# A cached-attention block on one core: one row in fourteen of the last weight matrix is loaded by a part of the DMA engines

## The chip, the core and the metric

The kernel runs on one core of one Trainium2 chip. Times are device microseconds (us) of whole executions; the figure for a kernel is the median of its runs. One execution was also taken with the hardware profiler: its span is counted from the first to the last instruction. TensorE (PE) multiplies matrices, VectorE (DVE) and ScalarE (ACT) work element by element, GpSimd (POOL) clears memory, SyncE (SP) issues the transfers, and 16 DMA engines move the data from memory (HBM) into the 128 partitions of the on-chip buffer.

## The reference, cut to what matters

A decoder block for 8 batch rows of width 512. Attention looks at the last 2048 keys of 8 cache heads in each of 8 batch rows (32 query heads of 128); its caches make up most of the bytes. Behind it stands an MLP: 512 to 1792 to 512, with a squared relu between. All is float32.

```
mod = (silu(c) @ w_mod).reshape(8, 6, 1, 512)      # sa, ca, ga, sb, cb, gb
h = layernorm(x) * (1 + ca) + sa
q = h @ wq                                          # 512 x 4096
o = softmax(q k^T / sqrt(128)) v                    # last 2048 positions of each cache
x = x + ga * (o @ wo)                               # 4096 x 512
h = layernorm(x) * (1 + cb) + sb
r = relu(h @ w1 + b1)                               # 512 x 1792
out = x + gb * ((r * r) @ w2 + b2)                  # 1792 x 512
```

## The kernel before

Every large array goes through four buffers, `slots`, of 128 partitions by 32 KB. A list `loads` (line 105) gives their order: w_mod and wq, then K and V of each batch row in two halves of 4 MB, then wo in two halves, w1 and w2. `pump` (line 115) hands the next entry to `load` (line 71) as soon as a slot is free, and `done` (line 120) frees one behind the last instruction that reads it. All these transfers are issued on SP's queue, in the order of the list, and a transfer waits at its issue for the slot's last readers. Two further things set when it is issued: the eight semaphores on which landings are counted go round, so a transfer also waits for the landing of the one eight issues before it.

The caches' middle part (lines 286 to 448) is a software pipeline over the eight batch rows: DVE transposes K in its slot (line 287), PE makes the scores (line 297), ACT the exponentials, PE the weighted sum of V (line 378). `qb` (line 206) are two buffers of 4 KB in a partition which hold the queries for line 297, spread with zeros; they are read last in the second half of the last batch row. The bytes of K, V, wo, w1 and w2 are spread over partitions so that every transfer into a slot has 128 of them.

What the change touches comes behind that. `wo` (line 453) is multiplied in two forms. Its first 16 row groups go 512 columns wide, four at a time into four groups of 32 columns of the array; their partial sums are copied to SBUF (lines 463 and 464) and folded in by line 467. The 16 others, loaded in pieces of 8, 4 and 4, go in the form of line 472: four matmuls of 128 columns for each row group. Then x1, its layernorm (`norm`, `scaled`) and the transposed `h2T` follow (lines 479 to 483).

The MLP: each partition holds four rows of w1 (`"(p kc) n -> p kc n"`), and 14 rows of w2 (`"(p c) n -> p c n"`). The first product has its 1792 columns cut in four parts of 448 (FG), one for each 32 columns of the array (line 494), after a matmul of four rows that puts the bias in (line 489). Relu, square and a transpose of 32 by 32 blocks (lines 505 to 507) run in two halves of seven, and make `rT`: 14 (FC) left operands of 128 by 32, one for each row of w2 in a partition. Line 516 multiplies each by its row of w2 in four parts of 128 columns, and y goes out (lines 524 to 526). w1 is loaded in two pieces (three of its four rows, then one) and w2 in pieces of 8, 4, 1 and 1 rows; PE waits for each piece by itself. b1 and b2 are loaded at the start, by POOL's queue.

## Time and profile before

| | |
|---|---|
| median of 3 runs | 394.1 us (393.8 to 394.24) |
| the profiled execution | 394.03 us, its span 392.2 us |
| mean granted TensorE clock in it | 0.839 |
| busy: PE, DVE, ACT, POOL | 65%, 55%, 11%, 1% of the span |
| moved by SP's queue (q1) | 164.69 MB in 6768 packets, 98.1% of the 16 engines' span |
| read from HBM | 164.77 MB, 420 GB/s over the span |

A row of a timeline gives start, duration, engine, line, operation, output and inputs, count, and in brackets how long the engine stood idle before it and for whom. A row of a table of windows gives the stretch, its length, the busy time of PE, PE's weight loads, DVE, ACT and POOL with the number of instructions, the granted TensorE clock, the share of the 16 DMA engines' time that was busy, and GB/s. PE shows two passes, so two instructions and two weight loads, for each float32 matmul of the source. The chain of waits is followed back from the last instruction.

### The profile page before, as it was taken

To read this page: it belongs to the slowest core of one execution; us is meant where nothing else is said; L and a number is where in the kernel's file an instruction comes from. 1 tells how busy PE (TensorE), PEld (TensorE's weight loads), DVE (VectorE), ACT (ScalarE), POOL (GpSimd) and SP (SyncE) were. 2 spreads that over 40 slices of the span, in tenths; PEclk is the share of its full clock that TensorE was granted. 3 is DMA by queue.
4 is the path that set the end of the run, shared out by engine and by line. 5 is a ranking of instruction groups with operands and counts; after the bars stand their busy time and mean duration, and the time that the engine had idled before them with its cause. 6 is when DMAs were issued, how large, how long until landed. Compare 5 with 4: busy or idle time off the path is not lost.

```text
span 392.2 us, 4985 instructions
## 1 busy us (share of the span) xinstructions
PE 254.6 (65%) x2224; PEld 112.9 (29%) x2224; DVE 213.8 (55%) x228; ACT 42.0 (11%) x88; POOL 4.7 (1%) x12
## 2 busy tenths in 40 slices
PE   0554808678966693849484939394849384984965
PEld 0211302051231332224332522143224221452423
DVE  2420299399394939283928491939293927230022
ACT  1300100030030002000200120003000300140000
POOL 4000000000000000000000000000000000000000
PEclk9998768969977988789578967797788879997869
DMA  8999999999999999999999999999999999999994
GB/s 333 429 428 426 431 441 438 431 434 438 426 431 426 428 426 428 428 433 434 429 434 433 438 427 428 434 433 428 426 428 434 424 431 426 438 429 412 433 417 170
DMA packets 6997, 165.15 MB, mean 421 GB/s; under 512 B 824, under 2 KB 1088, under 8 KB 1472
## 3 DMA queue, kind: packets, MB, share of 16 engines
q1 hardware_dynamic: 6768, 164.69, 98.1%
q8 instruction: 17, 0.28, 0.3%
q10 hardware_dynamic: 144, 0.13, 0.1%
q14 instruction: 4, 0.03, 0.0%
q0 software_dynamic: 64, 0.01, 0.0%
HBM read 164.77 MB, written 0.07 MB: 420 GB/s over the span
## 4 chain that ended last, share of the span: by engine, by line
DMA 55%; DVE 23%; PE 20%; issue 0%; ACT 0%; DVEq 0%; ACTq 0%
DMA slot<-in_A_k_cache_dram 37%; DVE slot L287 20%; PE s_ps L297 16%; DMA slot<-in_B_w_dram 8%; DMA slot<-in_A_v_cache_dram 6%; DMA xc_in<-in_xc_dram 3%; PE m_ps L221 2%; PE o_ps L378 2%; DVE pT L367 1%; PE t_ps L366 1%; PE t_ps L516 0%; DVE s L309 0%; DVE s L313 0%; DVE mx L318 0%; DVE e_sb L148 0%
## 5 line engine op out<-in xcount | busy, mean ns | idle before, releaser
L287 DVE STREAM_TRANSPOSE slot<-slot 128x2048 f32<-128x2048 f32 x64 | 144.0, 2284 | 43.4 <-DMA slot<-in_A_k_cache_dram 43.3
L297 PE MATMUL s_ps<-slot,qb 128*32 128x512 f32 x512 | 120.9, 1092 | 71.1 <-DVE slot L287 70.5
L297 PEld LDWEIGHTS s_ps<-slot,qb 128*32 128x32 f32 x512 | 24.2, 135 | 147.3 <-issue 79.0
L378 PE MATMUL o_ps<-slot,pT 128*32 128x256 f32 x1024 | 59.7, 381 | 0.8 <-DMA slot<-in_A_v_cache_dram 0.8
L378 PEld LDWEIGHTS o_ps<-slot,pT 128*32 128x32 f32 x1024 | 45.4, 112 | 29.1 <-issue 18.4
L366 PE MATMUL t_ps<-ident,prd 128*128 128x128 f32 x128 | 25.2, 348 | 17.3 <-ACT prd L356 9.5
L309 DVE STREAM_TRANSPOSE s<-s_ps 128x512 f32<-128x512 f32 x8 | 5.7, 717 | 54.1 <-PE s_ps L297 54.1
L366 PEld LDWEIGHTS t_ps<-ident,prd 128*128 128x128 f32 x128 | 18.5, 177 | 23.1 <-ACT prd L356 22.4
L356 ACT ACTIVATE prd<-pr,rz 128x512 f32<-128x512 f32 x32 | 20.5, 710 | 9.4 <-DVE rz L348 9.4
L332 ACT ACTIVATE pr<-s,nm 128x512 f32<-128x512 f32 x8 | 5.8, 722 | 142.7 <-DVE nm L326 142.7
L367 DVE TENSOR_TENSOR pT<-t_ps,m 128x512 f32<-128x512 f32 x32 | 20.2, 670 | 0.7 <-PE t_ps L366 0.6
L388 ACT COPY o_sb<-o_ps 128x256 f32<-128x256 f32 x16 | 5.8, 362 | 121.7 <-PE o_ps L378 121.7
L243 PE MATMUL t_ps<-slot,h1T 128*32 128x512 f32 x64 | 11.6, 889 | 10.2 <-DMA slot<-in_A_wq_dram 10.2
L255 DVE STREAM_TRANSPOSE qT<-t_ps 128x512 f32<-128x512 f32 x2 | 1.4, 717 | 19.0 <-PE t_ps L243 19.0
L274 DVE TENSOR_TENSOR qb<-qrep,block 128x512 f32<-128x512 f32 x8 | 9.0, 1124 | 2.1 <-ACT qrep L266 2.1
L158 PE MATMUL m_ps<-xsum,sel 128*128 128x1 f32 x2 | 0.6, 363 | 13.9 <-DVE xsum L181 13.9
L344 PE MATMUL m_ps<-z,same 128*128 128x1 f32 x16 | 3.3, 273 | 9.1 <-ACT pr L332 9.1
L453 PE MATMUL s_ps<-slot,oT 128*32 128x512 f32 x32 | 5.6, 864 | 5.2 <-DMA slot<-in_A_wo_dram 5.2
L243 PEld LDWEIGHTS t_ps<-slot,h1T 128*32 128x32 f32 x64 | 2.7, 155 | 18.6 <-issue 12.1
L221 PE MATMUL m_ps<-slot,cT 128*32 128x384 f32 x64 | 7.9, 665 | 0.0
L404 DVE TENSOR_TENSOR og<-m_ps,m 128x128 f32<-128x128 f32 x8 | 2.2, 272 | 8.9 <-PE m_ps L396 8.9
L494 PE MATMUL t_ps<-slot,h2T 128*32 128x448 f32 x32 | 5.6, 871 | 2.2 <-DMA slot<-in_B_w_dram 2.2
(93 smaller groups left out, 95.1 us busy)
## 6 DMA issues: line engine op xcount, KB each, us to landing
slot<-in_A_k_cache_dram SPq DMA_DIRECT2D x16, 4096.0 KB, 21.8
slot<-in_A_v_cache_dram SPq DMA_DIRECT2D x16, 4096.0 KB, 25.9
slot<-in_A_wq_dram SPq DMA_DIRECT2D x2, 4096.0 KB, 31.7
slot<-in_w_mod_dram SPq DMA_DIRECT2D x2, 3072.0 KB, 13.9
slot<-in_A_wo_dram SPq DMA_DIRECT2D x1, 4096.0 KB, 22.6
slot<-in_B_w_dram SPq DMA_DIRECT2D x1, 2688.0 KB, 27.8
slot<-in_A_wo_dram SPq DMA_DIRECT2D x1, 2048.0 KB, 25.7
slot<-in_A_wo_dram SPq DMA_DIRECT2D x2, 1024.0 KB, 28.2
```

What stands on the lines that cost most here:

```text
L221: nc.tensor.matmul(pm[i][32 * q : 32 * q + 32, : 3 * P].rearrange("p (m n) -> p m n", m=3), cT[:, kc, :], wm[:, 3 * i : 3 * i + 3, q, :], ...
L243: nc.tensor.matmul(pq[t][32 * x : 32 * x + 32, :], hT[:, kc, :], w[:, 2048 * t + 512 * x : 2048 * t + 512 * x + 512], start=(kc == 0), sto ...
L274: nc.vector.tensor_mul(qb[b % 2][:, :, :, :REP], qrep_b[:, :, None, :, b].to_broadcast([P, 32, 4, REP]), block[:, None, :, None].to_broadc ...
L287: nc.vector.transpose(k, k)
L297: nc.tensor.matmul(S_[b][32 * x : 32 * x + 32, :].rearrange("p (j i) -> p j i", i=8), q[:, n : n + 32], k[:, :, c, :, x], start=(t == 0 an ...
L309: nc.vector.transpose(s1.rearrange("p a j r -> p j a r"), S_.pop(b).rearrange("p (j i) -> p j i", i=32))
L332: nc.scalar.activation(pr.rearrange("p j (a i) -> p j a i", a=4), S2_.pop(b).rearrange("p (a j i) -> p j a i", a=4, i=8), AF.Exp, bias=NM_ ...
L356: nc.scalar.activation(d, pr[:, 4 * n : 4 * n + 4, :, None].to_broadcast([P, 4, 32, 4]), AF.Copy, scale=RZ_[b][0])
L366: nc.tensor.transpose(pp[:, P * i : P * i + P], d[:, i].rearrange("p i u -> p (i u)"), one)
L367: nc.vector.tensor_mul(PT_[b][:, n].rearrange("p q j (x r) -> p q (j x) r", r=REP), pp.rearrange("p (y q r) -> p q y r", y=16, r=REP), m16 ...
L378: nc.tensor.matmul(o[32 * (m % 4) : 32 * (m % 4) + 32].rearrange("p u d -> p (u d)"), PT_[b][:, n, 2 * q + t, 2 * u : 2 * u + 2, :].rearra ...
L388: nc.scalar.copy(O_[b][:, t], o)
```

## The change

w2's first 1664 rows are loaded as before, but 13 to a partition (FC is 13 and FG 416), in pieces of 6, 4, 1, 1 and 1. Its last 128 rows go to 32 partitions, four rows (8 KB) to each: 80 rows to partitions 0 to 19 and 48 rows to partitions 32 to 43. The access pattern of each of these two transfers has 5 and 3 as its outermost dimension; the change calls them loads of five and of three engines. They stand in SP's queue between w1 and the other pieces of w2. Their place is the memory of the two `qb` buffers, which are now one tile, `qb_all`; POOL clears 64 partitions of it behind the last scores (a memset of 64 by 2048), since the matmuls read 64 partitions.

w1 is loaded in four pieces instead of two. The 128 columns of w1 that belong to the extra rows of w2 have matmuls of their own, of 80 and of 48 columns, into another bank, `px`; relu, square and transpose of them make `rxT` with four left operands of 64 by 32, and 16 more matmuls of line 563 multiply them by `w2x` ahead of the others. Relu and square now run over 6 and 7 of the 13.

wo's form of 512 columns takes 28 row groups instead of 16, and the form of 128 columns the last four. b1 (in two parts) and b2 are issued on ACT's queue at the start, behind xc, instead of POOL's.

PE's program at wo, before (s_ps takes the form of 512 columns, m_ps that of 128; slot_81 holds wo's first half, slot_82 its second):

```order
L453 MATMUL s_ps<-slot_81,oT 32x512 x16
L467 MATMUL m_ps<-at_i,sel 32x128 x4
L472 MATMUL m_ps<-slot_82,oT 32x128 x64
L158 MATMUL m_ps<-x1sum,sel 128x1
L167 MATMUL m_ps<-ssq,sel 128x1
```

and the same place now (slot_84 and slot_85 are wo's halves):

```order
L470 MATMUL s_ps<-slot_84,oT 32x512 x16
L470 MATMUL s_ps<-slot_85,oT 32x512 x12
L484 MATMUL m_ps<-at_i,sel 32x128 x4
L489 MATMUL m_ps<-slot_85,oT 32x128 x16
L171 MATMUL m_ps<-x1sum,sel 128x1
L180 MATMUL m_ps<-ssq,sel 128x1
```

Twelve row groups went ahead of the fold, and 48 matmuls of 128 columns behind it became 12 of 512 ahead of it.

PE's program in the MLP, before (slot_84 is w1, slot_83 w2):

```order
L167 MATMUL m_ps<-ssq,sel 128x1
L489 MATMUL t_ps<-b_in,ident 32x448 x4
L494 MATMUL t_ps<-slot_84,h2T 32x448 x16
L511 MATMUL t_ps<-b_in,ident 32x128 x4
L516 MATMUL t_ps<-slot_83,rT 32x128 x56
```

and now (slot_87 is w1, slot_86 w2, qb_all the extra rows of w2; the three rows behind L511 stand four times, once for each row of w1):

```order
L507 MATMUL t_ps<-b_in,ident 32x416 x4
L511 MATMUL m_ps<-b_x,ident 32x80
L511 MATMUL m_ps<-b_x,ident 32x48
L520 MATMUL m_ps<-slot_87,h2T 32x80
L520 MATMUL m_ps<-slot_87,h2T 32x48
L528 MATMUL t_ps<-slot_87,h2T 32x416 x4
...
L556 MATMUL t_ps<-b_in,ident 32x128 x4
L563 MATMUL t_ps<-qb_all,rxT 32x128 x16
L563 MATMUL t_ps<-slot_86,rT 32x128 x52
```

The first product has ten matmuls more, the second twelve more, and the new sixteen stand first in the second.

SP's queue, its last transfers before with what each waits for (PE_49 is PE's count, a name with DMAHW an earlier landing; slot_82 is wo's second half, slot_84 w1, slot_83 w2):

```order
L99 DMA slot_82<-in_A_wo_dram 128x2048 [waits PE_49] x2
L99 DMA slot_84<-in_B_w_dram 128x5376 [waits DMAHW3_49,PE_49]
L99 DMA slot_84<-in_B_w_dram 128x1792 [waits PE_49]
L99 DMA slot_83<-in_B_w_dram 128x4096 [waits DMAHW4_49,PE_49]
L99 DMA slot_83<-in_B_w_dram 128x2048 [waits PE_49]
L99 DMA slot_83<-in_B_w_dram 128x512 [waits DMAHW5_49,PE_49]
L99 DMA slot_83<-in_B_w_dram 128x512 [waits DMAHW6_49,PE_49]
```

and now (slot_85 is wo's second half, slot_87 w1, qb_all and slot_86 w2):

```order
L112 DMA slot_85<-in_A_wo_dram 128x2048 [waits PE_49] x2
L112 DMA slot_87<-in_B_w_dram 128x1792 [waits DMAHW6_49,PE_49]
L112 DMA slot_87<-in_B_w_dram 128x1792 [waits PE_49] x2
L112 DMA slot_87<-in_B_w_dram 128x1792 [waits DMAHW7_49,PE_49]
L106 DMA qb_all<-in_B_w_dram 20x1x2048 [waits DMAHW0_49,Pool_49]
L106 DMA qb_all<-in_B_w_dram 12x1x2048 [waits DMAHW1_49]
L112 DMA slot_86<-in_B_w_dram 128x3072 [waits DMAHW2_49,PE_49]
L112 DMA slot_86<-in_B_w_dram 128x2048 [waits DMAHW3_49,PE_49]
L112 DMA slot_86<-in_B_w_dram 128x512 [waits DMAHW4_49,PE_49]
L112 DMA slot_86<-in_B_w_dram 128x512 [waits DMAHW5_49,PE_49]
L112 DMA slot_86<-in_B_w_dram 128x512 [waits DMAHW6_49,PE_49]
```

Eleven transfers stand where six stood, and the two of 20 and 12 partitions come ahead of the others of w2, and each still waits for the landing eight issues before it.

The diff, cut to its core:

```diff
@@ -41,8 +41,9 @@
     F = w1.shape[1]
     NJ = W // 32
     NQ = D // P
-    FG = F // NQ
-    FC = F // P
+    FC = F // P - 1
+    FG = FC * 32
+    FX = F - P * FC
     SCALE = float(DH) ** -0.5
     assert (B, HKV, D, DH, REP, NJ, NQ, F) == (8, 8, 512, 128, 4, 64, 4, 1792)
 
@@ -59,9 +60,16 @@
     x_in, c_in = xc_in[:, 0, :], xc_in[:, 1, :]
     nc.scalar.dma_start(xc_in, xc)
     b1_in = consts.tile([NQ, FG], F32, name="b1_in")
+    b1_x = consts.tile([1, FX], F32, name="b1_x")
     b2_in = consts.tile([NQ, P], F32, name="b2_in")
-    nc.gpsimd.dma_start(b1_in, b1.rearrange("(g n) -> g n", g=NQ))
-    nc.gpsimd.dma_start(b2_in, b2.rearrange("(g n) -> g n", g=NQ))
+    nc.scalar.dma_start(b1_in, b1[: P * FC].rearrange("(g n) -> g n", g=NQ))
+    nc.scalar.dma_start(b1_x, b1[P * FC :].rearrange("(g n) -> g n", g=1))
+    nc.scalar.dma_start(b2_in, b2.rearrange("(g n) -> g n", g=NQ))
+
+
+    EXTRA = ((0, 5, P * FC, 0), (32, 3, P * FC + 80, 80))
+    qb_all = consts.tile([P, 2, 32, 4, 8], F32, name="qb_all")
+    w2x = qb_all.rearrange("p t n a z -> p (t n a z)")
 
     slots = [consts.tile([P, NJ * DH], F32, name=f"slot{i}") for i in range(SLOTS)]
     free = list(range(SLOTS))
@@ -90,10 +98,15 @@
             pieces = [(lo - 16 * key[1], v[:, lo:hi]) for lo, hi in cuts]
         elif kind == "w1":
             v = w1.rearrange(r_kc, p=P)
-            pieces = [(0, v[:, :3]), (3, v[:, 3:])]
+            pieces = [(i, v[:, i : i + 1]) for i in range(NQ)]
         else:
-            v = w2.rearrange("(p c) n -> p c n", p=P)
-            pieces = [(lo, v[:, lo:hi]) for lo, hi in ((0, 8), (8, 12), (12, 13), (13, 14))]
+
+            for g, o, first, _ in EXTRA:
+                v = w2[first : first + 16 * o].rearrange("(i o c) n -> o i (c n)", i=4, o=o)
+                nc.sync.dma_start(w2x[g : g + 4 * o, :], v)
+            v = w2[: P * FC].rearrange("(p c) n -> p c n", p=P)
+            cuts = ((0, 6), (6, 10), (10, 11), (11, 12), (12, 13))
+            pieces = [(lo, v[:, lo:hi]) for lo, hi in cuts]
         for lo, v in pieces:
             a, n = v.shape[1:]
             nc.sync.dma_start(t[:, lo * n : (lo + a) * n].rearrange("p (a n) -> p a n", n=n), v)
@@ -203,9 +216,11 @@
     nc.vector.tensor_copy(same, own[:, :, None, :].to_broadcast([P, 4, 4, 8]))
     sel4 = consts.tile([P, 32, 4], F32, name="sel4")
     nc.vector.tensor_copy(sel4, sel[:, :32, None].to_broadcast([P, 32, 4]))
-    qb = [consts.tile([P, 32, 4, 8], F32, name=f"qb{i}") for i in range(2)]
+    qb = [qb_all[:, i] for i in range(2)]
     for t in qb:
         nc.gpsimd.memset(t, 0.0)
+    rx = consts.tile([64, 32, 4], F32, name="rx")
+    nc.gpsimd.memset(rx, 0.0)
     oT = consts.tile([P, 32, 32], F32, name="oT")
     nc.gpsimd.memset(oT, 0.0)
     mx = consts.tile([P, 32], F32, name="mx")
@@ -301,6 +316,8 @@
                     start=(t == 0 and c == 0),
                     stop=(t == 1 and c == 3),
                 )
+        if b == B - 1 and t == 1:
+            nc.gpsimd.memset(w2x[:64, :], 0.0)
         done(("K", b, t))
 
     def rows(b):
@@ -449,13 +466,13 @@
 
 
     wo_ps = ps_s.tile([P, D], F32, name="s_ps")
-    for i in range(16):
+    for i in range(28):
         nc.tensor.matmul(
             wo_ps[32 * (i % 4) : 32 * (i % 4) + 32, :],
             oT[:, i, :],
-            slot(("wo", 0), D)[:, i, :],
+            slot(("wo", i // 16), D)[:, i % 16, :],
             start=(i < 4),
-            stop=(i >= 12),
+            stop=(i >= 24),
         )
     x1 = consts.tile([P, P], F32, name="x1")
     x1sum = work.tile([P, 1], F32, name="x1sum")
@@ -467,7 +484,7 @@
         nc.tensor.matmul(
             pw[32 * q : 32 * q + 32, :P], sel[:, :32], at_i[:, q * P : (q + 1) * P], start=True, stop=False
         )
-    for i in range(16, 32):
+    for i in range(28, 32):
         for q in range(NQ):
             nc.tensor.matmul(
                 pw[32 * q : 32 * q + 32, :P],
@@ -485,11 +502,28 @@
     w1t = slot(("w1",), F)
     w2t = slot(("w2",), D)
     ph = ps_t.tile([P, 512], F32, name="t_ps")
+    px = bank()
     for g in range(NQ):
         nc.tensor.matmul(
             ph[32 * g : 32 * g + 32, :FG], one[:NQ, g : g + 1].to_broadcast([NQ, 32]), b1_in, start=True, stop=False
         )
+    for g, o, _, at_ in EXTRA:
+        nc.tensor.matmul(
+            px[g : g + 32, : 16 * o],
+            one[:1, :1].to_broadcast([1, 32]),
+            b1_x[:, at_ : at_ + 16 * o],
+            start=True,
+            stop=False,
+        )
     for kc in range(NQ):
+        for g, o, first, _ in EXTRA:
+            nc.tensor.matmul(
+                px[g : g + 32, : 16 * o],
+                h2T[:, kc, :],
+                w1t[:, kc, first : first + 16 * o],
+                start=False,
+                stop=(kc == NQ - 1),
+            )
         for g in range(NQ):
             nc.tensor.matmul(
                 ph[32 * g : 32 * g + 32, :FG],
@@ -498,11 +532,22 @@
                 start=False,
                 stop=(kc == NQ - 1),
             )
+
+    for g, o, _, _ in EXTRA:
+        nc.scalar.activation(
+            rx[g : g + 32, : 4 * o, :].rearrange("p (o i) c -> p i o c", i=4),
+            px[g : g + 32, : 16 * o].rearrange("p (i o c) -> p i o c", i=4, o=o),
+            AF.Relu,
+        )
     r = work.tile([P, 32, FC], F32, name="relu", tag="a")
     rT = work.tile([P, FC, 32], F32, name="rT", bufs=1)
+    rxT = work.tile([64, 4, 32], F32, name="rxT", bufs=1)
     h = ph[:, :FG].rearrange("p (l c) -> p l c", l=32)
-    for lo, hi in ((0, 7), (7, 14)):
-        nc.scalar.activation(r[:, :, lo:hi], h[:, :, lo:hi], AF.Relu)
+    nc.scalar.activation(r[:, :, :6], h[:, :, :6], AF.Relu)
+    nc.vector.tensor_mul(rx, rx, rx)
+    nc.vector.transpose(rxT, rx.rearrange("p l c -> p c l"))
+    nc.scalar.activation(r[:, :, 6:], h[:, :, 6:], AF.Relu)
+    for lo, hi in ((0, 6), (6, FC)):
         nc.vector.tensor_mul(r[:, :, lo:hi], r[:, :, lo:hi], r[:, :, lo:hi])
         nc.vector.transpose(rT[:, lo:hi], r[:, :, lo:hi].rearrange("p l c -> p c l"))
 
@@ -511,14 +556,16 @@
         nc.tensor.matmul(
             py[32 * q : 32 * q + 32, :P], one[:NQ, q : q + 1].to_broadcast([NQ, 32]), b2_in, start=True, stop=False
         )
-    for f in range(FC):
+    chunks = [(rxT[:, c, :], w2x[:64, D * c : D * c + D]) for c in range(4)]
+    chunks += [(rT[:, f, :], w2t[:, f, :]) for f in range(FC)]
+    for f, (left, right) in enumerate(chunks):
         for q in range(NQ):
             nc.tensor.matmul(
                 py[32 * q : 32 * q + 32, :P],
-                rT[:, f, :],
-                w2t[:, f, q * P : (q + 1) * P],
+                left,
+                right[:, q * P : (q + 1) * P],
                 start=False,
-                stop=(f == FC - 1),
+                stop=(f == len(chunks) - 1),
             )
     y = work.tile([P, P], F32, name="y", bufs=1)
     nc.vector.tensor_mul(y, py[:, :P], mods[1][:, 2, :])
```

## The prediction

> **What bounds the kernel now.** I read the page first: is the core waiting for data or for an engine?
>
> ```profile
> span 392.2 us, 4985 instructions
> ...
> PE 254.6 (65%) x2224; PEld 112.9 (29%) x2224; DVE 213.8 (55%) x228; ACT 42.0 (11%) x88; POOL 4.7 (1%) x12
> ...
> q1 hardware_dynamic: 6768, 164.69, 98.1%
> q8 instruction: 17, 0.28, 0.3%
> ```
>
> No engine is near full, and SP's queue q1 keeps the 16 DMA engines busy for 98.1% of the span: the kernel is a stream of 164.69 MB with a tail behind it. The bytes stay the same, so only the end of the stream and the tail can change. Next the last pieces of the chain of waits (start, length, what):
>
> ```profile
> 354.51 32.83 DMA slot<-in_B_w_dram
> 387.34 0.04 issue
> 387.38 1.75 PE t_ps L516 x48
> 389.13 0.02 issue
> 389.15 0.30 DVE y L524
> 389.48 0.29 DVE y L525
> ```
>
> The end hangs on landings of w2. A window table of the last microseconds says how the stream ends; its last two columns are the busy share of the DMA engines and GB/s.
>
> ```profile
> 380.00:383.00 3.00, 3.00 (x24) 0.90 (x16) 0.00 (x0) 0.00 (x0) 0.00 (x0) 0.54 0.98 415
> 383.50:384.50 1.00, 0.37 (x11) 0.10 (x8) 0.47 (x2) 0.62 (x2) 0.00 (x0) 1.00 0.96 385
> 384.50:385.00 0.50, 0.00 (x0) 0.00 (x0) 0.50 (x2) 0.00 (x0) 0.00 (x0) 1.00 0.85 340
> 385.00:385.50 0.50, 0.46 (x17) 0.47 (x21) 0.47 (x2) 0.00 (x0) 0.00 (x0) 1.00 0.70 291
> 385.50:386.00 0.50, 0.50 (x28) 0.50 (x23) 0.36 (x1) 0.00 (x0) 0.00 (x0) 1.00 0.53 221
> 386.00:386.50 0.50, 0.50 (x29) 0.50 (x23) 0.00 (x0) 0.00 (x0) 0.00 (x0) 1.00 0.53 213
> ...
> 387.00:387.50 0.50, 0.12 (x4) 0.12 (x8) 0.00 (x0) 0.00 (x0) 0.00 (x0) 1.00 0.53 205
> 387.50:388.00 0.50, 0.50 (x24) 0.50 (x26) 0.00 (x0) 0.00 (x0) 0.00 (x0) 1.00 0.37 123
> 388.00:388.50 0.50, 0.50 (x28) 0.41 (x16) 0.00 (x0) 0.00 (x0) 0.00 (x0) 1.00 0.01 4
> ```
>
> The share falls to 0.53 at about 385.3 and stays there until 387.5: some seven or eight engines have done their equal shares 2.5 to 3 us before the other eight. An engine's rate hardly rises when the others stop: 415 GB/s over 0.98 x 16 engines is 26.5 GB/s for each, 213 over 0.53 x 16 is 25.1. So the end is set by what the late half still has to move. The page's 17 instruction fetches (0.3% of 16 x 392.2 is 18.8 us, 1.1 us each) could be what holds single engines back; the page does not name engines.
>
> How close the engines follow stands in the timeline of the MLP:
>
> ```profile
> 375.80 0.40 DVE L142 STREAM_TRANSPOSE h2T<-h_sb 128x128 f32<-128x128 f32 x1
> ...
> 377.95 5.58 PE L494 MATMUL t_ps<-slot,h2T 128*32 128x448 f32 x32 [2.18 <-DMA slot<-in_B_w_dram]
> ...
> 383.59 0.62 ACT L505 ACTIVATE relu<-t_ps 128x224 f32<-128x224 f32 x2 [8.40 <-PE t_ps L494]
> ...
> 384.43 0.56 DVE L507 STREAM_TRANSPOSE rT<-relu 128x224 f32<-128x224 f32 x1
> 384.91 0.35 DVE L506 TENSOR_TENSOR relu<-relu 128x224 f32<-128x224 f32 x1
> ...
> 385.04 1.95 PE L516 MATMUL t_ps<-slot,rT 128*32 128x128 f32 x64 [1.16 <-DVE rT L507]
> ...
> 388.66 0.16 PEld L516 LDWEIGHTS t_ps<-slot,rT 128*32 128x32 f32 x8 [0.24 <-DMA slot<-in_B_w_dram]
> ```
>
> PE starts the last row of w2 at 388.66, 0.24 us after it ran dry, so that row landed at 388.62 (0.04 of issue, as at 387.34), and PE needs 0.47 more, to 389.13.
>
> **The change part by part.** *The row that the late half no longer loads.* One row of w2 in each of an engine's 8 partitions is 16 KB (16,384 bytes); at 25.1 to 26.5 GB/s that is 0.62 to 0.65 us. I take 0.62: the last landing would come 0.62 earlier if the late half gets nothing else.
>
> *The two loads of 20 and 12 partitions.* Each gives an engine four times 8 KB, 32 KB, which is 1.24 us. If both start from the same first engine, three engines get two of them, 2.48, less the 0.62: 1.86 us more than now (on eight different engines it would be 0.62 more; I take the dearer). The seven or eight early engines end at 384.5 to 385.5; with 1.86 they end at 386.4 to 387.4, still ahead of a late half at 388.0. Hidden, and the cover is thin: an engine must now end 1.3 us or more before the last one (1.86 against a last landing that comes 0.5 earlier). [...]
>
> *More pieces.* w1 and w2 come in nine pieces of 128 partitions instead of six. The chain has the third piece of w2 landing at 387.34 minus two rows: from 387.34 to 388.62 two one-row pieces took 1.28, 0.64 each, 0.02 above the rate. I take 0.1 for three pieces more and the shorter runs of w1. Bounds: 0, since the bytes are the same, and 0.3, since 25.1 against 26.5 GB/s is 5%, and three rows of w1 are some 6.4 us of the stream. Nothing speaks for a gain beyond the bytes.
>
> *wo.* Twelve row groups change their form. The rows, in order of the two forms and the landing that the second waits for:
>
> ```profile
> 361.67 5.61 PE L453 MATMUL s_ps<-slot,oT 128*32 128x512 f32 x32 [5.21 <-DMA slot<-in_A_wo_dram]
> ...
> 366.24 0.13 PEld L453 LDWEIGHTS s_ps<-slot,oT 128*32 128x32 f32 x4 [0.29 <-issue]
> ...
> 367.35 0.42 DVE L463 COPY at_i<-s_ps 128x256 f32<-128x256 f32 x1 [10.16 <-PE s_ps L453]
> ...
> 368.38 2.89 PE L472 MATMUL m_ps<-slot,oT 128*32 128x128 f32 x94
> ...
> 371.45 1.08 PE L472 MATMUL m_ps<-slot,oT 128*32 128x128 f32 x32 [0.19 <-DMA slot<-in_A_wo_dram]
> ```
>
> At the full clock 94 passes of the narrow form take 2.89 (32 for four row groups: 0.98), and four row groups of the wide one, two weight-load groups of 0.42 (0.13 and 0.29 of idle before it), 0.84. Twelve groups in the wide form take 2.5 us, so PE would reach the fold at about 369.8 (367.28 now), have copied and folded 1.1 us later (368.38 now), and stand ready at 370.9 for the last four groups, which wait for the same landing as now (371.45 less 0.04). Then 1.08 as before: x1 and h2T (ready at 376.20) do not move. The cover is 0.5 us; beyond it x1 would be late by what the fold is.
>
> *w1 in quarters.* Now PE waits 2.18 us for three rows of w1 at once, to 377.95. A quarter is 0.92 MB, 2.1 us of the stream, so the first two have landed at about 373.7 and 375.8, and PE starts with h2T, at 376.25. A row of w1 took 5.58 / 4, most of it at half the clock: the weight loads of L494 follow each other every 0.75, 1.49 for a row. The 80 extra columns lengthen the busiest group of 32 columns of the array from 448 to 496, so 1.65 at half the clock and 0.83 at full. Two rows end at 379.55, the others at 381.2 (full clock, the fourth row landing at 380.05) to 382.9 (half): 0.6 to 2.3 before the 383.53 of now. Relu, square and transpose of the extra columns add at most 0.62 on ACT and 0.35 + 0.56 on DVE, by the rows above for larger tiles. In the quick case `rxT` is there at about 382.8 and rT by 384.7, ahead of w2. In the slow one `rxT` comes at 384.5, and PE's 16, 24 and 16 matmuls (0.061 each by 1.95 for 32) end at 387.9; with two rows more it is 388.4, and PE would start the last row 0.2 behind its landing. I take the quick case. The gain in front ends at w2's landings either way.
>
> *POOL and ACT.* The memset of 64 partitions by 2048:
>
> ```profile
> L208 POOL MEMSET qb<- 128x1024 f32 x2 | 1.8, 946 | 0.0
> ```
>
> and from the timeline ACT's first issue and wait, and SP's issues of w1 and w2:
>
> ```profile
> 0.74 0.40 ACTq L60 DMA_DIRECT2D xc_in<-in_xc_dram  x1
> ...
> 11.38 0.31 ACT L146 ACTIVATE e_sb<-xc_in 128x128 f32<-128x128 f32 x1 [8.93 <-DMA xc_in<-in_xc_dram]
> ...
> 350.05 16.78 SPq L99 DMA_DIRECT2D slot<-in_B_w_dram  x6
> ```
>
> 1.9 us by 0.946 for 1024, behind the last scores, on an engine with nothing else to do; SP's queue reaches the extra loads only behind w1, which it issues from 350.05. The three small loads on ACT's queue cost some 0.4 each behind xc, before ACT's idle 8.93. Nothing. SP's waits for landings stay ahead of the engines: its last issue of now ended at 366.83, 21 us before the end.
>
> *Sum.* -0.62 + 0.1 + nothing is -0.52: last landing 388.1, PE's end 388.6, span 391.7. The profiled execution took 394.03 with its span of 392.2, and the runs have a median of 394.1; so 393.5 for a profiled one and **393.6** as the median. That is 0.13%, less than the 0.2% that a measurement of this kernel can tell from no change. Its own bounds are 0.62 to 0.65, 0 to 0.3 and 0 to 0.2 for PE, with the runs' spread of 0.2 about it: 393.2 to 394.1.
>
> **The rivals.** *Late engines get the loads (slower).* If one of the three engines with both loads belongs to the late half, it ends 1.86 + 0.1 later than now: 396.1. If only the fourth or fifth does, 1.24 - 0.62 + 0.1 = 0.7: 394.8. It decides as soon as a loaded engine now ends after some 386.8. For it: the rows name no engine, and half of them are late. Against: five neighbours would have to straddle the halves, and an early half that holds together fits the sharp step from 0.85 to 0.53. 0.15 and 0.06.
>
> *PE falls to half the clock in the last stretch.* The granted clock goes by how busy PE was just before:
>
> ```profile
> 372.52:375.93 3.41, 1.63 (x14) 0.75 (x12) 1.97 (x9) 0.76 (x3) 0.00 (x0) 1.00 0.95 398
> ...
> 375.90:379.30 3.40, 1.35 (x8) 0.45 (x12) 0.30 (x1) 0.00 (x0) 0.00 (x0) 0.50 1.04 437
> 379.40:382.70 3.30, 3.30 (x24) 1.12 (x20) 0.00 (x0) 0.00 (x0) 0.00 (x0) 0.50 0.99 422
> 382.80:386.10 3.30, 2.14 (x56) 1.22 (x52) 1.79 (x4) 0.62 (x2) 0.00 (x0) 1.00 0.82 336
> ```
>
> A stretch of 3.4 us with 1.63 of PE is followed by half the clock, a full one by the whole. With w1 done early, PE has at most 16 + 24 matmuls at 0.06, 2.4 us, in the stretch from 382.8, and less where the first 16 come sooner (1.5): at that edge. At half the clock the 28 matmuls that wait for w2's later rows take 3.4 instead of 1.7 from 386.2 and end at 389.6, 0.5 after the 389.13 of now: 394.6. [...] 0.11.
>
> *It gains more.* PE's program has 14 matmuls less, so instruction fetches come at other times. If the engine that ends last loses the one fetch of 1.1 us ahead of its end, the next late engine binds; the share of 0.37 in 387.5 to 388 spreads the late engines' ends over some 0.4 us. Then 0.52 + 0.4 less, 393.2. 0.16.
>
> *It does not do what it says.* If the late half is held back by something shared, the bytes moved elsewhere free nothing, and 0.1 of pieces stays: 394.2. The unchanged rate for each engine speaks against it. 0.06.
>
> **How the numbers follow.** The forecast keeps 0.46. 393.0 to 394.9 leaves out 396.1 alone (0.15) and little else. Faster by over 0.2% (under 393.3): 0.16 and a tail of 0.03. Slower (over 394.9): 0.15 and 0.04 of the case at 394.8. The rest, 0.62, lies within: 0.43 of the forecast, 0.11, 0.06, 0.02 of 394.8.
>
> **What would show it.** Right: the DMA share stays above 0.53 to 387 and falls in one step; PE starts the first product near 376.25 and the last row of w2 near 388.15. Wrong: a loaded engine last, seen in PE's wait for the extra rows and in a thin share of 0.06 to 0.2 to 390; or PE still busy when the last row lands, at a granted clock of 0.5.

## The result, and the profile after

The changed kernel took 391.84 us as the median of 6 runs (391.69 to 393.19), the kernel before beside it 393.96 us (393.74 to 394.24): a ratio of 0.9949, with a 95% interval from 0.9938 to 0.996. It is 2.1 us faster; the prediction had 0.5. The page of the changed kernel:

```profile
span 390.1 us, 4950 instructions
...
PE 254.9 (65%) x2196; PEld 110.9 (28%) x2196; DVE 214.8 (55%) x230; ACT 42.5 (11%) x90; POOL 5.4 (1%) x12
...
q1 hardware_dynamic: 7240, 164.70, 98.3%
```

The bytes are those of before, and the span is 2.1 us shorter. The end of the chain of waits (start, length, what):

```profile
349.10 27.14 DMA slot<-in_B_w_dram
...
376.30 10.25 DMA slot<-in_B_w_dram
386.55 0.04 issue
386.59 0.47 PE t_ps L563 x8
387.06 0.02 issue
387.08 0.30 DVE y L571
```

The last row of w2 lands at 386.55 instead of 388.62, and PE ends 0.51 behind it, as before. So all of the gain lies in the stream. How it ends, in the windows (last two columns: busy share of the DMA engines, GB/s):

```profile
380.00:383.00 3.00, 2.73 (x66) 1.55 (x62) 2.11 (x6) 1.02 (x4) 0.00 (x0) 0.96 0.98 412
...
384.50:385.00 0.50, 0.32 (x12) 0.35 (x16) 0.00 (x0) 0.00 (x0) 0.00 (x0) 1.00 0.78 299
385.00:385.50 0.50, 0.50 (x28) 0.50 (x24) 0.00 (x0) 0.00 (x0) 0.00 (x0) 1.00 0.71 270
385.50:386.00 0.50, 0.50 (x27) 0.37 (x16) 0.00 (x0) 0.00 (x0) 0.00 (x0) 1.00 0.45 172
386.00:386.50 0.50, 0.25 (x8) 0.00 (x0) 0.00 (x0) 0.00 (x0) 0.00 (x0) 1.00 0.13 37
```

The long shelf at 0.53 is gone: the share stays at 0.7 to 0.8 and falls within a microsecond. But the stream was ahead long before its end. The transfers up to wo are the same in both kernels, and PE starts wo when its first half lands:

```profile
360.19 6.39 PE L470 MATMUL s_ps<-slot,oT 128*32 128x512 f32 x44 [5.03 <-DMA slot<-in_A_wo_dram]
```

That is 360.19 against 361.67 before, 1.48 us earlier, at a place where no row of w2 has moved. The 300 us ahead of it, before and then after:

```profile
40.00:340.00 300.00, 203.91 (x1593) 88.31 (x1587) 193.24 (x172) 29.30 (x63) 0.00 (x0) 0.82 1.00 430
```

```profile
40.00:340.00 300.00, 204.41 (x1610) 87.18 (x1606) 194.21 (x173) 29.32 (x63) 1.80 (x1) 0.83 1.00 432
```

Both have the engines busy all the time, and one moves 430 GB/s, the other 432. The trace's packets say the same more sharply: of the 4480 packets of 32 KB, 4451 took 1.213 us each in the changed kernel; before, only 1178 did. Nearly all the others took 1.215 to 1.219 in the changed kernel and 1.214 to 1.228 before; 19 in each took 1.45 us or more.

### The profile page after: what moved, and what is told of

It reads as the page before. It is cut to its first block, busy times and chain, and to the rows that moved or that the text cites. A ratio compares the mean times of both kernels' runs of the same rounds, so it can differ in the third digit from the quotient of the medians.

```text
span 390.1 us, 4950 instructions
## 1 busy us (share of the span) xinstructions
PE 254.9 (65%) x2196; PEld 110.9 (28%) x2196; DVE 214.8 (55%) x230; ACT 42.5 (11%) x90; POOL 5.4 (1%) x12
## 4 chain that ended last, share of the span: by engine, by line
DMA 55%; DVE 23%; PE 20%; ACT 1%; issue 1%; DVEq 0%; ACTq 0%; SPq 0%
DMA slot<-in_A_k_cache_dram 43%; DVE slot L302 20%; PE s_ps L312 16%; DMA slot<-in_B_w_dram 10%; DMA xc_in<-in_xc_dram 3%; PE m_ps L236 2%; PE t_ps L383 1%; PE o_ps L395 1%; DVE pT L384 1%; ACT prd L373 0%; DVE s L326 0%; DVE s L330 0%; DVE mx L335 0%; DVE e_sb L161 0%; ACT pr L349 0%
## 5 line engine op out<-in xcount | busy, mean ns | idle before, releaser
L312 PE MATMUL s_ps<-slot,qb_all 128*32 128x512 f32 x512 | 121.3, 1094 | 70.5 <-DVE slot L302 70.4
L312 PEld LDWEIGHTS s_ps<-slot,qb_all 128*32 128x32 f32 x512 | 23.2, 136 | 147.8 <-issue 80.1
L395 PE MATMUL o_ps<-slot,pT 128*32 128x256 f32 x1024 | 60.6, 383 | 0.4 <-DMA slot<-in_A_v_cache_dram 0.4
L395 PEld LDWEIGHTS o_ps<-slot,pT 128*32 128x32 f32 x1024 | 44.6, 113 | 30.3 <-issue 18.5
L258 PE MATMUL t_ps<-slot,h1T 128*32 128x512 f32 x64 | 10.7, 829 | 11.3 <-DMA slot<-in_A_wq_dram 11.3
L470 PE MATMUL s_ps<-slot,oT 128*32 128x512 f32 x56 | 7.9, 709 | 5.4 <-DMA slot<-in_A_wo_dram 5.4
L289 DVE TENSOR_TENSOR qb_all<-qrep,block 128x512 f32<-128x512 f32 x8 | 8.9, 1117 | 2.2 <-ACT qrep L281 2.2
L236 PE MATMUL m_ps<-slot,cT 128*32 128x384 f32 x64 | 6.7, 582 | 0.0
```

The costliest lines, as they stand in the source:

```text
L236: nc.tensor.matmul(pm[i][32 * q : 32 * q + 32, : 3 * P].rearrange("p (m n) -> p m n", m=3), cT[:, kc, :], wm[:, 3 * i : 3 * i + 3, q, :], ...
L258: nc.tensor.matmul(pq[t][32 * x : 32 * x + 32, :], hT[:, kc, :], w[:, 2048 * t + 512 * x : 2048 * t + 512 * x + 512], start=(kc == 0), sto ...
L289: nc.vector.tensor_mul(qb[b % 2][:, :, :, :REP], qrep_b[:, :, None, :, b].to_broadcast([P, 32, 4, REP]), block[:, None, :, None].to_broadc ...
L312: nc.tensor.matmul(S_[b][32 * x : 32 * x + 32, :].rearrange("p (j i) -> p j i", i=8), q[:, n : n + 32], k[:, :, c, :, x], start=(t == 0 an ...
L395: nc.tensor.matmul(o[32 * (m % 4) : 32 * (m % 4) + 32].rearrange("p u d -> p (u d)"), PT_[b][:, n, 2 * q + t, 2 * u : 2 * u + 2, :].rearra ...
L470: nc.tensor.matmul(wo_ps[32 * (i % 4) : 32 * (i % 4) + 32, :], oT[:, i, :], slot(("wo", i // 16), D)[:, i % 16, :], start=(i < 4), stop=(i ...
```

## The experiments

The queue of the biases and the place of the slots are the two things that the change alters ahead of wo. `qb_all` and `b1_x` now stand ahead of the slots, so the first slot starts at byte 28416 of a partition instead of 19840: 8192 bytes more for `qb_all`, 512 for `b1_x`, and 128 less because `b1_in` is shorter.

**Biases on ACT's queue alone** (in the kernel before), and **back on POOL's** (in the changed one):

```diff
-    nc.gpsimd.dma_start(b1_in, b1.rearrange("(g n) -> g n", g=NQ))
+    nc.scalar.dma_start(b1_in, b1.rearrange("(g n) -> g n", g=NQ))
```

> The kernel before, with b1 and b2 loaded by ACT's queue instead of POOL's; nothing else. Theory 1, POOL's two small loads slow the whole stream: the first landing of the transfers between 47 and 348 us comes up to 1.4 us earlier, as it does in the changed kernel, and the time falls from 394.0 to 392.5 us. Theory 2, the place of the four slots in a partition decides the stream's rate: no change, 394.0 us. Theory 3, each program finds its data in memory in another place and no edit decides it: no forecast.

> The changed kernel, with b1 (both parts) and b2 loaded by POOL's queue as before. Theory 1: the 1.4 us are lost again, 393.3 us, and the gain over the kernel before is the row's 0.65 alone. Theory 2: no change against the changed kernel, 391.85 us.

394.13 us, ratio 1.0002 (0.9994 to 1.0011); and 392.17 us, 0.9962 (0.995 to 0.9975). The queue of the biases is worth nothing that this tells: theory 1 falls.

**The slots moved, nothing else:**

```diff
+    qb = [consts.tile([P, 32, 4, 8], F32, name=f"qb{i}") for i in range(2)]
+    pad = consts.tile([P, 96], F32, name="pad")
     slots = [consts.tile([P, NJ * DH], F32, name=f"slot{i}") for i in range(SLOTS)]
```

> The kernel before, with its four slots where the changed kernel has them (8576 bytes further up in each partition: the queries' two buffers and a pad of 384 bytes come ahead of them). Theory 1: 394.0 us as before. Theory 2: 392.5 us.

392.32 us, 0.9958 (0.9946 to 0.997): theory 2. PE's start of wo in it:

```profile
360.03 5.26 PE L455 MATMUL s_ps<-slot,oT 128*32 128x512 f32 x32 [5.11 <-DMA slot<-in_A_wo_dram]
```

**Alignment or distance:** the kernel before with a pad of 32 elements (128 bytes), with `qb` ahead of the slots and no pad, and with a pad of 16 elements:

```diff
+    pad = consts.tile([P, 32], F32, name="pad")
     slots = [consts.tile([P, NJ * DH], F32, name=f"slot{i}") for i in range(SLOTS)]
```

> The kernel before with a pad of 128 bytes ahead of its slots. In the kernel before the first slot starts at byte 19840 of a partition, a multiple of 128 and not of 256; in the changed one at 28416, a multiple of 256 and not of 512; here at 19968, a multiple of 512. The alignment theory (a start at a multiple of 256 lets every transfer of 32 KB in a partition take 1.213 us) expects 392.3 us, as with the slots moved by 8576 bytes. If 512 gives more than 256, it is less than 392.1. The distance theory (it is the place far up that counts, not the alignment) expects 394.0.

> The kernel before with the queries' two buffers ahead of the slots and no pad: the first slot starts at byte 28032, far up as in the changed kernel, and a multiple of 128 and not of 256, as in the kernel before. The alignment theory expects 394.0 us, the distance theory 392.3.

> The kernel before with a pad of 64 bytes ahead of its slots: the first starts at byte 19904, a multiple of 64 and not of 128. Alignment theory: no better than a multiple of 128, so 394.0 us or above; if each halving of the alignment costs as much as the last, some 395.6. If it is something else about byte 19840 than its alignment, 392.3.

And the changed kernel with a pad of 32 elements:

> The changed kernel with a pad of 128 bytes ahead of its slots, so that the first starts at byte 28544 of a partition: a multiple of 128 and not of 256, as in the kernel before. Alignment theory: the 1.4 us of the stream's rate are lost, 391.9 becomes 393.3 us; what is left against 394.0 is the row. If the slots' place mattered only together with something else of the kernel before, 391.9.

| first slot at byte | multiple of | kernel | us | ratio (interval) |
|---|---|---|---|---|
| 19840 | 128 | before | 393.9 to 394.0 | 1 |
| 19904 | 64 | before, pad | 394.18 | 1.0008 (0.9999 to 1.0016) |
| 19968 | 512 | before, pad | 392.38 | 0.9956 (0.9944 to 0.9969) |
| 28032 | 128 | before, `qb` ahead | 393.95 | 0.9997 (0.9988 to 1.0006) |
| 28416 | 256 | before, `qb` ahead, pad | 392.32 | 0.9958 (0.9946 to 0.997) |
| 28416 | 256 | changed | 391.84 | 0.9949 (0.9938 to 0.996) |
| 28544 | 128 | changed, pad | 393.52 | 1.0006 (0.9994 to 1.0017) |

The start of wo with 28032 bytes, and in the changed kernel with 28544:

```profile
361.57 5.00 PE L453 MATMUL s_ps<-slot,oT 128*32 128x512 f32 x24 [4.77 <-DMA slot<-in_A_wo_dram]
```

```profile
361.26 5.35 PE L472 MATMUL s_ps<-slot,oT 128*32 128x512 f32 x24 [5.01 <-DMA slot<-in_A_wo_dram]
```

Between these starts it is alignment and not distance: in the kernel before, the two at multiples of 256 bytes are worth 1.6 us (392.32 and 392.38 against 393.96), the one at 512 among them no more, and 64 costs no more than 128 that the intervals tell. Over 40 to 340 us, the three kernels that start at a multiple of 256 or 512 moved 432 GB/s, the four others 430 or 431. A pad moves the small tiles behind the slots too; the packets that differ are those into the slots. They account for most of it: an engine's 280 packets of 32 KB take 341.25 us in sum before and 340.22 in the changed kernel, 1.0 less, and the instruction fetches among them are shorter too (1.07 us on average before, 0.93 after; some two for each engine that carries them, so 0.3). Of the 1.48 at the start of wo some 0.2 stay open. (Five of the 12 runs of the last row took 394.8 to 395.2; what can part runs so comes below.)

**Only w2's extra rows** of the change, and then **wo alone undone**:

```diff
-            pieces = [(i, v[:, i : i + 1]) for i in range(NQ)]
+            pieces = [(0, v[:, :3]), (3, v[:, 3:])]
...
-    for i in range(28):
+    for i in range(16):
```

(The first kernel has both edits and the biases on POOL's queue, the second the edit of wo.)

> The changed kernel with wo in two forms of 16 row groups, w1 in two pieces and b1 and b2 on POOL's queue, all as before: of the change only w2's extra rows remain (and the slots' place). Theory 1: 393.3 us, as for the changed kernel with POOL's loads, since wo's form and w1's pieces are worth nothing. Theory 2: 391.85 us. A time above either by 0.3 or more would show that w1's quarters or wo's form carry part of the gain.

> The changed kernel with wo alone as before (16 row groups in the wide form, 16 in the narrow one); w1 stays in quarters and the biases on ACT's queue. Fetch theory: PE's program has 36 matmuls more, its 17th instruction fetch comes at some 380 us, ahead of the stream's end, and the time is 393.1 us, as with 36 idle matmuls put in. If w1 in quarters or ACT's loads carry part of the gain, it lies between 391.9 and 392.8.

393.31 us, 0.9982 (0.9974 to 0.9991), and 392.99 us, 0.9977 (0.9968 to 0.9986). With the slots in place already, the extra rows alone make the kernel slower, by 1.0 against 392.32, and wo's form, priced at nothing, is worth 1.1 to 1.5. Where the first of the two kernels loses it, in windows of its end:

```profile
385.50:386.00 0.50, 0.12 (x5) 0.15 (x9) 0.00 (x0) 0.00 (x0) 0.00 (x0) 1.00 0.31 119
386.00:386.50 0.50, 0.50 (x24) 0.50 (x24) 0.00 (x0) 0.00 (x0) 0.00 (x0) 1.00 0.10 37
386.50:387.00 0.50, 0.50 (x27) 0.41 (x16) 0.00 (x0) 0.00 (x0) 0.00 (x0) 1.00 0.18 57
387.00:387.50 0.50, 0.46 (x16) 0.16 (x8) 0.00 (x0) 0.00 (x0) 0.00 (x0) 1.00 0.03 12
```

A share of about 0.06 is one engine of sixteen: a single engine is still at work while the other fifteen are done. The last landing's semaphore has 16 increments in the trace, and the changed kernel's loads of five and of three engines land with 5 and 3; so the increments are read as the engines' ends, in us behind the first of them:

```
before        385.13 + 0 .21 .22 .30 .32 .66 .81 1.99 2.86 2.96 2.99 3.06 3.09 3.21 3.28 3.49
changed       383.10 + 0 .18 .26 1.66 2.37 2.65 2.69 2.85 2.91 2.98 3.10 3.18 3.19 3.19 3.31 3.44
w2 rows alone 383.08 + 0 .24 .27 1.89 2.59 2.60 2.77 2.78 2.82 2.87 2.98 3.00 3.05 3.34 3.38 4.53
```

What holds that one engine, the next experiments show, is one more instruction fetch: a packet of 16,384 bytes on a queue of its own (q8). That it brings PE's program is read from its time, which moves with the number of PE's instructions; that one of the same 16 engines carries it, from the landings below. The fetches up to 385 us, in the changed kernel and then with w2's rows alone, where the 17th comes at 381.48:

```profile
q8 instruction: 16, 0.26, 0.2%
```

```profile
q8 instruction: 17, 0.28, 0.3%
```

**The number of PE's instructions, nothing else:** 36 idle matmuls more in the changed kernel; and 36 less, far from the end, in the kernel with w2's rows alone.

```diff
     gather(B - 1)
+    idle = bank()
+    for _ in range(36):
+        nc.tensor.matmul(idle[:32, :1], one[:, :32], one[:, :1], start=True, stop=True)
```

> The changed kernel with 36 matmuls of one column more, 144 instructions of PE, in the 5 us in which PE waits for wo behind the last batch row; nobody reads what they write. That is as many instructions as the wide form of wo saved. Fetch theory (PE's 17th instruction fetch, at 381.5 us when only w2's change is made and at 386.1 in the changed kernel, costs the DMA engine that it rides on some 1.2 us just ahead of the stream's end): the 17th fetch comes back to about 381 us and the time rises from 391.8 to 393.0. Work theory (wo's wide form or w1 in quarters gained the 1.1 us because PE is ready earlier): 391.8, since the 36 lie in idle time.

```diff
         for m in range(32):
+            if b == 0 and 4 <= m < 22:
+                continue
```

> Only w2's extra rows of the change (wo in two forms of 16, w1 in two pieces, the biases on POOL's queue), and in the first batch row 18 of the 32 matmuls in each half of the weighted sum of V are left out: 144 instructions of PE less, 300 us ahead of the end. Fetch theory: PE's 17th fetch comes only at about 386 us instead of 381.5, and the time falls from 393.3 to 392.1. Work theory: 393.3, since nothing near the end has changed.

393.03 us, 0.9969 (0.9957 to 0.9981), and 392.17 us, 0.9953 (0.994 to 0.9965). Both as the fetch theory had it: 144 instructions in idle time cost 1.2 us, and 144 fewer, 300 us ahead of the end, give 1.1 back. The fetches up to 385 us:

```profile
q8 instruction: 17, 0.28, 0.3%
```

```profile
q8 instruction: 16, 0.26, 0.2%
```

The landings show that here a fetch counts wherever in the kernel it comes, and that the engine which carried one stayed behind: in the kernel before, after the first fetch at 32.11, one engine ends 1.60 us behind the first at the landing of 38.92, and still 1.61 at that of 77.77; the others end within 0.6. In that kernel, the 16 engines' ends of three transfers, in us behind the first of them:

```
landed  fetches
 28.17    0    0 .09 .10 .11 .12 .16 .19 .22 .23 .30 .34 .39 .40 .50 .57 .58
194.83    7    0 .01 .02 .09 .18 .25 .37 .41 1.07 1.38 1.49 1.50 1.61 1.76 1.83 1.99
377.81   16    0 .19 .23 .33 .35 .65 .81 2.03 2.92 2.98 3.02 3.04 3.12 3.28 3.35 3.56
```

Without a fetch all engines end within 0.6 us. After seven, eight engines are a step (1.07 to 1.99) behind: one of them, by its time, for a packet of 8 KB on queue q14 at 83.19, since a second engine is 1.18 behind at the landing of 87.49, ahead of the second fetch at 87.80. After sixteen, eight are two steps (2.92 to 3.56) behind. So the late half that the prediction saw goes back to PE's fetches, two on each of eight engines, and a 17th ahead of the end puts one engine three steps behind (the 4.53 above). The trace does not name engines; that the eight take turns is read from these counts.

The clock adds to it in the profile with 36 more, that of its slowest run (393.6). There w2's last row lands at 387.67, 1.1 later than in the changed kernel, but PE had fallen to half the clock and ends 1.07 behind it instead of 0.5:

```profile
384.50:385.00 0.50, 0.50 (x20) 0.26 (x11) 0.00 (x0) 0.00 (x0) 0.00 (x0) 0.73 0.75 291
...
386.00:386.50 0.50, 0.50 (x12) 0.50 (x16) 0.00 (x0) 0.00 (x0) 0.00 (x0) 0.50 0.06 25
```

The profile with wo undone has the same: a landing 0.66 later (387.21), and PE 0.94 behind it. So in that kernel the fetch is only a part of the loss; with w2's rows alone the clock was full to the end.

**The row undone in the changed kernel**, and the same with PE kept busy:

```diff
+    idle = bank()
+    for i in range(12):
+        nc.tensor.matmul(idle[32 * (i % 4) : 32 * (i % 4) + 32, :448], h2T[:, i % 4, :], w1t[:, i % 4, :448], start=True, stop=True)
     py = ps_t.tile([P, 512], F32, name="t_ps")
```

> The changed kernel without w2's extra rows: w2 has 14 rows to a partition as before, with all that belongs to it in the MLP, while wo's 28 and 4, w1 in quarters, ACT's loads and the slots at byte 28416 stay. The step of the prediction on the row (16 KB less for each late engine, 0.62 us, against 0.1 for the pieces) expects the stream to end 0.5 to 0.65 later than in the changed kernel: 392.4 us. If the two loads to a part of the engines gain nothing, 391.9.

> The changed kernel without the extra rows, as measured at 393.4 us, with 12 matmuls of w1's form more (448 columns, read by nobody) in the 3.7 us in which PE stood idle between the products of the MLP. Clock theory (PE stood at half the clock from 384.6 on because it had been idle, and ended 1.42 us behind w2's last landing instead of 0.5): the granted clock is 1.00 from 383 on, PE ends 0.5 behind the landing, and the time is 392.4, so that the row itself is worth 0.4 to 0.6. If the clock is not the cause, the time stays at 393.4 and the row is worth 1.5.

393.43 us, 0.9986 (0.9976 to 0.9995), and 392.65 us, 0.9956 (0.9944 to 0.9968). The first is the prediction's second rival in the flesh. Its last product, and two windows with the granted clock (third column from the right):

```profile
383.42 4.93 PE L518 MATMUL t_ps<-slot,rT 128*32 128x128 f32 x112 [3.70 <-DMA slot<-in_B_w_dram]
```

```profile
383.00:385.00 2.00, 1.58 (x48) 1.61 (x52) 0.00 (x0) 0.00 (x0) 0.00 (x0) 0.84 0.68 281
385.00:387.00 2.00, 2.00 (x45) 1.97 (x41) 0.00 (x0) 0.00 (x0) 0.00 (x0) 0.50 0.37 137
```

and the second window with the gap filled:

```profile
385.00:387.00 2.00, 1.60 (x56) 1.13 (x45) 0.00 (x0) 0.00 (x0) 0.00 (x0) 1.00 0.38 141
```

PE stood idle for 3.7 us, fell to half the clock, and ended 1.4 us behind a landing at 386.96. Filled, it ends 0.5 behind one at 386.95. Against that the changed kernel's 386.55 makes the row worth 0.4 of the stream, and its second profile below, with a landing at 386.20, 0.75. The times leave as much room: by the ratios 0.2 to 0.3, by the medians, whose kernels before were 0.3 apart, 0.8. In the changed kernel the extra rows' own 32 passes stand in that gap.

**w1 in two pieces** (the lines above), **w1 in halves**, and the changed kernel once more beside the latter:

```diff
-            pieces = [(i, v[:, i : i + 1]) for i in range(NQ)]
+            pieces = [(0, v[:, :2]), (2, v[:, 2:])]
```

> The changed kernel with w1 alone as before, in two pieces. The prediction's step (w1 in quarters lets PE start earlier, but w2's landings set the end): 391.8 us, or 0.1 less for two transfers fewer. If the earlier start is what keeps PE off the path at the end, 392.5 or more.

> The changed kernel with w1 in two halves of two rows. With w1 in three rows and one, w2's last row landed at 386.20 us instead of 386.55, but PE came late to it and ended at the same time. If each transfer less is worth 0.1 to 0.17 on the stream and PE can start w1 with the first half, landed before h2T is ready, PE ends 0.3 earlier than in the changed kernel: 391.5 us. If the 0.35 was the scatter of one execution, 391.8.

> The changed kernel once more, on the same chip as the one with w1 in halves: 391.8 us by its first measurement, 0.9949 of the kernel before.

391.85 us, 0.9934 (0.9921 to 0.9947); 393.22 us, 0.9971 (0.996 to 0.9982); 391.85 us, 0.9952 (0.994 to 0.9964). By the times quarters are worth nothing, as predicted. (In the profile with two pieces the last row landed at 386.20 and PE, late with w1, ended 0.76 behind it; the changed kernel's second profile also has 386.20, so the 0.35 against its first is scatter.) The halves met neither forecast. Their runs fall in two groups: four at 391.87 to 391.96, seven at 393.22 to 393.51. One run of the changed kernel in six is like the second group (393.19, and 393.34 here). In the halves' profiled run, of the second group, the 17th fetch came at 385.67, and one engine ended 1.48 us behind the next to last. But in the changed kernel's second profile, one of the quick runs (391.54), it came at 385.65, and no engine ended late. So the moment of the fetch alone does not part the groups; which engine carries it, and what that engine still has to move, may, and no trace here shows it.

**The 17th fetch a little earlier:** 8 idle matmuls instead of the 36.

> The changed kernel with 8 idle matmuls of one column more (32 instructions of PE) in the 5 us in which PE waits for wo. In the changed kernel the 17th instruction fetch came at 385.7 to 386.1 us, just as the late engines end, and one run in six took 1.4 us longer. Edge theory: 32 instructions bring the fetch forward by some 0.5 us, so that it meets an engine that still has its last rows to move, and most runs take 393.2 to 393.4. If the odd runs have another cause, the median stays at 391.85.

392.56 us, 0.9959 (0.9943 to 0.9974): three runs at 391.6 to 392.0, three at 393.1 to 393.6. The second group is half of six runs now, against two of twelve in the changed kernel: too few to show that the 32 instructions did it, and "most" did not come. Nor does the 17th fetch come earlier in the profiled run, one of the second group: it starts at 386.08, as in the changed kernel's first profile. The stream is later in it, with a first engine done at 383.67 instead of 383.10 and 327 packets of 32 KB over 1.213 us instead of 29. The late engine in its windows:

```profile
386.00:386.50 0.50, 0.50 (x23) 0.26 (x12) 0.00 (x0) 0.00 (x0) 0.00 (x0) 1.00 0.42 148
386.50:387.00 0.50, 0.17 (x8) 0.00 (x0) 0.00 (x0) 0.00 (x0) 0.00 (x0) 1.00 0.00 0
387.00:387.50 0.50, 0.00 (x0) 0.00 (x0) 0.00 (x0) 0.00 (x0) 0.00 (x0) 1.00 0.09 12
387.50:388.00 0.50, 0.00 (x0) 0.00 (x0) 0.00 (x0) 0.00 (x0) 0.00 (x0) 1.00 0.03 8
```

The stream is done by 386.5 but for one engine, which moves its last rows from 387 on; PE waits for them. The other single runs of that group have no trace: that the same holds for them is argued.

**One row further, by eight engines:**

```diff
-    FC = F // P - 1
+    FC = F // P - 2
...
-    EXTRA = ((0, 5, P * FC, 0), (32, 3, P * FC + 80, 80))
+    EXTRA = ((0, 8, P * FC, 0), (32, 8, P * FC + 128, 128))
```

> The changed kernel carried one row further: 12 rows of w2 to each partition, and the last 256 rows to 64 partitions by two loads of eight engines each, so that eight engines get two loads and each engine one row less; a pad keeps the slots at a multiple of 256. By the sum of the prediction, if all of the eight are engines that end early (0 to 0.75 us behind the first, against 2.8 to 3.4 for the late ones): another 0.5 less, 391.3 us. If one or more of the eight belong to the late ones, that one ends 2.48 - 0.62 later than now, and the time is 393.5 or more.

394.12 us, 0.9996 (0.9985 to 1.0007). The engines' ends, as above:

```
two rows      382.72 + 0 .22 2.28 2.34 2.42 2.45 2.68 2.72 2.76 2.84 2.85 2.97 3.27 4.35 5.02 5.16
```

Three engines end 1.1 to 1.9 us behind the rest, which fits the expectation's case that some of the eight are late ones; that it is these, and how many, the trace does not name. (That eight engines carry each load is read from the changed kernel's two, of 5 and 3 for the outermost dimension, which land with 5 and 3 increments.) Then PE, starved, comes to half the clock on top:

```profile
385.50:386.00 0.50, 0.00 (x0) 0.00 (x0) 0.00 (x0) 0.00 (x0) 0.00 (x0) 0.78 0.21 82
386.00:386.50 0.50, 0.49 (x12) 0.46 (x16) 0.00 (x0) 0.00 (x0) 0.00 (x0) 0.50 0.20 78
```

No version tried is faster than the changed kernel by more than the intervals tell.

## Why the prediction was wrong

By the medians, the change divides like this:

| step | us | difference |
|---|---|---|
| before | 393.94 | |
| slots at a multiple of 256 | 392.32, 392.38 | -1.6 |
| and w2's extra rows | 393.31 | +1.0 |
| and wo in 28 and 4, biases on ACT | 391.85 | -1.5 |
| and w1 in quarters: the changed kernel | 391.84, 391.85 | 0 |

By the ratios the last two differences are -1.9 and +0.6, with intervals of about 0.5 about each kernel. Against the kernel before with its slots moved, the changed kernel is 0.5 faster (392.32 to 391.84), the forecast's 0.52; but the two intervals overlap, and the agreement is in part luck, since it holds a loss of 1.0 and a gain of 1.1 to 1.5 that stood in no term.

**The step that failed** is in the first part: "The bytes stay the same, so only the end of the stream and the tail can change." The rate changed too. The small tiles ahead of the slots changed, and this moved every large transfer's destination to a multiple of 256. `qb_all` alone, with its 8192 bytes, would not have done it (28032, no gain); the 384 bytes of the two parts of b1 did, 512 for `b1_x` less 128 for the shorter `b1_in`. The prediction followed what these tiles hold and when they are loaded, but not what they do to the slots' address. Worth 1.6 of the 2.1.

**The row** was right in kind: the last landing came 0.4 to 0.75 earlier for it (386.95 to 386.55 and 386.20), where the sum had 0.62. Without the row, w1 in quarters lands w2's last row at 386.96 and 386.95, in two pieces at 386.75 and 386.77 (in kernels that differ in wo's form too): 0.2 for pieces, within their bounds of 0 to 0.3. (The landing at 387.34 was that of w2's second piece, not its third; the 0.64 for a one-row piece is right.) What the sum missed is the price of its matmuls: 22 more (10 and 12) bring the 17th fetch from 386.28 to 381.48, ahead of the stream's end, and the row alone is a loss of 1.0.

**The two loads** are hidden, as said: the first rival fell, and the changed kernel's last engine is 3.44 behind the first as before (3.49), so the five engines must be early ones. That both loads start from the same engine, the dearer case, the trace after bears out: their 32 packets of 8 KB (0.309 us each) form three rows of eight, of 2.45 us each, and two of four, and each of the three increments of the second load (377.43, 377.71, 378.17) comes 1.17 to 1.19 behind one of the five of the first (376.26, 376.52, 376.76, 376.98, 378.26). The cover was worked out wrongly, though: with 1.86 more against a last landing 0.52 earlier, a loaded engine must have ended 2.4 us ahead of the last one (by 386.2), not 1.3. The seven early engines ended at 385.13 to 385.94 in the kernel before, so it held, by 0.3. With eight engines the time is what that rival's condition gives.

**wo** was called nothing. Its times were right: from the last landing of wo to h2T it is 4.75 us before and after (371.45 to 376.20, 369.82 to 374.57):

```profile
368.98 0.82 PE L484 MATMUL m_ps<-at_i,sel 128*32 128x128 f32 x8 [0.55 <-DVE at_i L480]
...
369.82 0.81 PEld L489 LDWEIGHTS m_ps<-slot,oT 128*32 128x32 f32 x32 [0.30 <-DMA slot<-in_A_wo_dram]
...
374.17 0.40 DVE L155 STREAM_TRANSPOSE h2T<-h_sb 128x128 f32<-128x128 f32 x1
...
374.77 0.34 PE L520 MATMUL m_ps<-slot,h2T 128*32 128x80 f32 x2
```

The cover of 0.5 was thinner than said: the fold ends at 369.80, and the last groups start at 369.82. What was not seen is that 36 matmuls are 144 instructions, and they keep the fetches before the end (up to 385 us) at 16. The third rival had the 14 matmuls less and the fetch of a late engine, as a gain over before. The runs show the other side: before and after both have 16, and wo's form only pays for what the row would have cost.

**w1, POOL and ACT** were right: nothing. PE started w1 at 374.77 and the last row at 386.59; both are the forecast's 376.25 and 388.15 less the 1.5 of the stream's lead, within 0.1.

**Half the clock** did not come in the profiled run (1.00 from 383 on), but it was not far: it came at 383.9 to 385.8, for 3.4 us (without the row from 384.4 to 387.8), in the profiles of five kernels beside it. It cost 0.9 us without the row, some 0.5 with wo undone and 0.6 with the 36 idle matmuls, came with late landings in the kernel of two rows, and cost nothing in the changed kernel with a pad, where the clock was back before the last row.

Open: why the rate of before suffers only from some 37 us on (until then 238 of 260 packets of 32 KB took 1.213 us there too), what decides which engine a fetch falls on, and whether the scattered single runs are all fetches.

## What to carry to other kernels

Where a stream of DMA is the bound, look up where each large tile starts in its partition before and after an edit. Here the starts at a multiple of 256 bytes were the quick ones, and a tile allocated ahead of the slots was enough to gain 1.6 us (0.4%; 393.96 to 392.38, by 128 bytes) or to lose 1.7 (391.84 to 393.52, by the same). Count the instruction fetches of PE's program up to the end of the stream: here each left one DMA engine behind to the end, wherever in the kernel it came, and the one that started a third round over the eight engines cost some 1.1 us, whatever the instructions did (393.31 to 392.17 with 144 fewer, 391.84 to 393.03 with 144 idle ones more). And an edit that gains by its mechanism can lose by its instruction count, so test it without its companions.

## What the runs showed of the hardware

A packet of 32 KB took 1.213 us in the changed kernel, whose first slot starts at a multiple of 256 bytes, and 1.217 on average in the kernel before, where it starts at one of 128 (the 19 of 1.45 us or more left out in each): 0.3% more. A start at one of 64 (byte 19904) was no worse than that: 430 GB/s over 40 to 340 us and the start of wo at 361.55, against 430 and 361.67 in the kernel before and 432 and 360.19 in the changed one. Why these starts differ, no run shows.

The changed kernel has 4392 instructions of PE, weight loads among them, and 17 packets of 16 KB on q8, one to some 258 instructions. Such a packet took 0.88 to 1.11 us in the two kernels, and its engine did not make it up: in the kernel before one fetch left an engine 1.38 to 1.99 us behind the first, two 2.92 to 3.56; with w2's rows alone a third left one 4.53. In the chain of waits that ends the changed kernel PE waits for no fetch; what a fetch cost was the data behind it on its DMA engine (1.2 us with the 36 idle matmuls).
